# Attention blocks on one Trainium2 core: V loaded from ScalarE's queue, wo by column halves, wq and the second x in small pieces, remainder tiles of 90 steps transposed by DMA

## The chip, the cores and the metric

The kernel runs on one core of one Trainium2 chip. TensorE (PE in the profile) does the matmuls, VectorE (DVE), ScalarE (ACT) and GpSimd (POOL) work beside it, and SyncE (SP) issues most DMAs. The metric is the device time of one execution in microseconds (us); lower is better.

## The reference: what is computed

Two independent grouped-query attention blocks, A and B, of the same shape; their outputs stand side by side in the last dimension. Everything is bf16.

```python
B, Sq, D = 16, 80, 576
Hq, Hkv, Sk, Dh = 32, 16, 512, 128
q = (x @ wq).reshape(B, Sq, Hq, Dh).transpose(0, 2, 1, 3)
k = jnp.repeat(k_cache, 2, axis=1)
v = jnp.repeat(v_cache, 2, axis=1)
scores = jnp.einsum("bhqd,bhkd->bhqk", q, k) * (Dh ** -0.5)
p = softmax(scores, axis=-1)
o = jnp.einsum("bhqk,bhkd->bhqd", p, v)
out = o.transpose(0, 2, 1, 3).reshape(B, Sq, Hq * Dh) @ wo
```

Each K and V head serves two query heads, that is 160 query rows (2 x 80) against 512 keys.

## The kernel before

**Units and tiles.** A unit U is one batch row with four K/V heads; there are 64 units in each problem, 128 in all (A is U = 0 to 63). A unit's 4 x 160 query rows make five tiles of 128 rows: tiles k = 1 to 4 hold the first 128 rows of each head, and the remainder tile k = 0 holds the last 32 rows of all four. A tile's work: scores of 128 x 512 by PE (line 658; line 644 for the remainder, four matmuls of 32 columns of the array side by side), the row maximum by VectorE (667), the exponential with row sums by ScalarE (671), a reciprocal by VectorE (677), the scaling of P by GpSimd (680), and four 128 x 128 transposes by PE (686) with a copy out of PSUM by VectorE (692 for the remainder, 694 for the others). P transposed (pT) is then multiplied with V (line 731, four matmuls of 160 columns for a head), and ScalarE copies the product to oT (747).

**The remainder tile by DMA.** In some units the four transposes and the copy of tile k = 0 are replaced by one DMA transpose from p_sb into pT (line 698), issued by SyncE. `RDMA`, `RPER` and `RSKIP` choose the units: U from 24 to 125 with U % 4 equal to 1 or 3, without 50 to 61, 45 in all. In these units the reciprocal is made in two parts, tile 0 alone and tiles 1 to 4 together (`RG`).

**Around the units.** Eight units share a q projection (an "octet"): 16 groups of five matmuls (540) whose results ScalarE or VectorE copy to qT (551, 552). Its wq part, 576 x 1024, is loaded for every second octet (lines 514 and 517), and used for both halves of the batch. Every 32 units a block of 16 heads of oT is multiplied with wo in 20 output blocks of 128 x 288 (line 781, 16 matmuls each), two column halves (c3) for each of ten row blocks (r); before, the two halves of a row block follow each other. The first result of a problem goes to acc, the last is added to acc (809) and stored (815). x of problem A is transposed by PE, x of problem B by four DMA transposes (481, 485).

**What sets the order.** The order on every engine is written out ahead by a planner (`_Sched`) in the program: every operation has a key (its wished time in steps), a stream in which order is kept, a duration, the buffers that it reads and writes, and for a DMA a `cost`. `arrange` plays the operations through on a model of the engines, with one DMA queue for all (`dma_free`) and a landing time `DLAT`; each engine takes the operation with the smallest key among those that are ready. `finalize` turns the buffers' dependences into semaphore waits. Scores run `LA` = 10 tiles ahead of the products. There are 5 buffers for K, 4 for V, 3 for pT, 12 for P.

**Queues.** SyncE issues all loads (K by DMA transpose at line 612, V by plain DMA at 616, wo in four parts of four heads at 580, wq, x), the remainder transposes and the stores, in one queue. ScalarE issues only the first four wq pieces.

The lines that the change and the steps below touch:

Of the kernel before, what the change touches and what calls it, by code (L numbers as in the profile page):

```python
# [22 lines left out]
KC = 2.95  # L23
VK = 8.0
KK = 8.0
DLAT = 1.6
XC = 0.4
QL2 = 10.0
VC = 1.65
WQC = 3.2  # L30
NQ = 3
NWS = 4
# [6 lines left out]
NML = 12  # L39
XDMA = True  # L40
RG = (((0, 1, 2, 3, 4),), ((0,), (1, 2, 3, 4)))
RDMA = (24, 126)
RPER = (1, 3)
RSKIP = ((50, 62),)
XK = (15.0, 15.0)
WQK = 4.0
WQKB = 4.0
RDC = 0.78
# [11 lines left out]
XH = -2.0  # L60
WQ1 = -16.8
OPX = ((12.0, 1.8), (18.5, 1.45), (18.5, 1.45), (18.5, 1.45))
# [3 lines left out]
WOL = 1.2  # L66
WOA = (99.0, 99.0, 99.0, 99.0)
WOS = 1.0
# [19 lines left out]
class _Op:  # L88
    __slots__ = ("engs", "eng", "key", "seq", "emit", "reads", "writes", "dsem", "stream", "dur", "lat", "cost",
                 "alloc", "pri", "after", "pre", "start", "done", "mode",  # L90
                 "deps", "signals", "sidx", "waits", "clock", "name")


class _Sched:
# [10 lines left out]
    def add(self, eng, key, emit, reads=(), writes=(), dsem=None, name="", stream=None, dur=0.1, lat=0.15,  # L105
            cost=0.0, alloc=(), mode=0, ahead=0.0, after=None):
# [5 lines left out]
        op.after = after  # L112
        op.seq = len(self.ops)
# [21 lines left out]
    def arrange(self):  # L135
        ops = sorted(self.ops, key=lambda o: (o.key, o.seq))
        last_w, readers = {}, {}
        for op in ops:
# [19 lines left out]
            op.pre = list(deps.values())  # L158
        streams = {}
# [11 lines left out]
        dma_free = 1.4  # L171
# [14 lines left out]
        def ready(o, now):  # L186
            t = 0.0
            if o.after is not None:
                d = self.marks[o.after]
                if d.start is None:  # L190
                    return None
                t = d.start
            for d in o.pre:
                if d.done is None:
                    return None
                if not (d.eng == "pe" and o.engs[0] == "pe"):
                    t = max(t, d.done)
            if o.alloc:
# [6 lines left out]
        while left:  # L205
# [30 lines left out]
            if o.dsem is not None:  # L236
                d0 = max(st + 0.5, dma_free)
                dma_free = d0 + o.cost
                o.done = dma_free + DLAT
            else:  # L240
                o.done = st + dur + o.lat
# [82 lines left out]
def bass_concat_heads__gqa_block_cached__gqa_block_cached__near_ridge_kernel(  # L324
# [27 lines left out]
    with ExitStack() as es:  # L352
# [11 lines left out]
        wo_sb = sb("wo_sb", [128, NWS * (HH // NWC), D], BF16)  # L364
# [10 lines left out]
        sem_names = (["e_pe", "e_act", "e_dve", "e_pool", "d_x00", "d_x01", "d_x10", "d_x11", "d_wo",  # L375
# [100 lines left out]
        for half in range(NPP):  # L476
            x_ap = probs[1][0]

            def em_ldxt(e, x_ap=x_ap, half=half):
                src = x_ap.rearrange("b s d -> (b s) d")[half * NROW:(half + 1) * NROW, :]  # L480
                return e.dma_start_transpose(xT[:, half, 0:4, :], src[:, 0:512].rearrange("n (c d) -> n c d", c=4))

            def em_ldxt4(e, x_ap=x_ap, half=half):
                src = x_ap.rearrange("b s d -> (b s) d")[half * NROW:(half + 1) * NROW, :]
                return e.dma_start_transpose(xT[:, half, 4:5, :],
                                             src[:, D - 128:D].rearrange("n (c d) -> n c d", c=1))

            k_ = 5.0 * (UPR + 16 * half - lead[NG // 2 + 2 * half]) - XK[half]
            S.add("sp", k_, em_ldxt, writes=[R(("xT", half, b_), 1) for b_ in range(NRT)], dsem="d_x%d0" % half,
                  name="ldxt%d" % half, stream="x", dur=4.7, cost=3.5)  # L490
            S.add("sp", k_ + 0.01, em_ldxt4, writes=[R(("xT", half, "t"), 1)], dsem="d_x%d0" % half,
                  name="ldxtb%d" % half, stream="x", dur=1.4, cost=0.9)

        QB = ((0, 6), (6, 2))
        for goct in range(NG):
# [7 lines left out]
            for pi, (c0, c1) in enumerate(pieces):  # L503
                t_ld = 5.0 * (u0 - lead[goct]) - (WQKB if goct == NG // 2 else WQK)
                if goct < 2:
                    t_ld = (-90.0, WQ1)[goct] + (10.0, 0.02)[goct] * pi
                fr = (c1 - c0) / 1024.0
                dsem = "d_wqs" if goct == 0 and pi == 0 else "d_wqt" if goct == 1 and pi == 0 else "d_wq%d" % wsl
                eng = "act" if goct == 0 else "sp"
                strm = "wqa" if goct == 0 else "wq"  # L510

                def em_ldwa(e, wq_ap=wq_ap, q=q, wsl=wsl, c0=c0, c1=c1):
                    src = wq_ap[0:512, q * 1024 + c0:q * 1024 + c1]
                    return e.dma_start(wq_sb[:, wsl, 0:4, c0:c1], src.rearrange("(c p) n -> p c n", p=128))

                def em_ldwb(e, wq_ap=wq_ap, q=q, wsl=wsl, c0=c0, c1=c1):
                    return e.dma_start(wq_sb[64:128, wsl, 4, c0:c1],
                                       wq_ap[512:576, q * 1024 + c0:q * 1024 + c1])

                wr = [pi] if len(pieces) == 2 else [0, 1]  # L520
                S.add(eng, t_ld, em_ldwa, writes=[R(("wq", wsl, "a", p_), wv) for p_ in wr], dsem=dsem,
                      name="ldwa%d.%d" % (goct, pi), stream=strm, dur=0.5, cost=WQC * fr)
                S.add(eng, t_ld + 0.01, em_ldwb, writes=[R(("wq", wsl, "b", p_), wv) for p_ in wr], dsem=dsem,
                      name="ldwb%d.%d" % (goct, pi), stream=strm, dur=0.5, cost=0.6 * fr)

            for i in range(8):
                for c in range(2):
# [27 lines left out]
                    if prob:  # L555
                        xr.append(R(("xT", half, "t"), 1))
                    S.add("pe", x, em_qp,
                          reads=[R(("wq", wsl, s_, i // 4), wv) for s_ in "ab"] + [R(("wqz",), 0)] + xr,
# [9 lines left out]
        for prob in range(2):  # L568
            wo_ap = probs[prob][4]
            hc = HH // NWC  # L570
            for hh in range(NPAIR):
                for wc in range(NWC):
# [322 lines left out]
```

## Time and profile before

| | |
|---|---|
| median of 3 runs | 782.39 us (781.14 to 784.07) |
| the profiled execution | 780.9 us |
| its span, first to last instruction | 779.2 us |
| PE busy | 772.0 us, 99% of the span |
| VectorE busy | 678.6 us, 87% |
| ScalarE busy | 611.6 us, 78% |
| GpSimd busy | 432.4 us, 55% |
| DMA moved | 166.44 MB, mean 214 GB/s |
| SyncE's queue (q1), share of the 16 DMA engines' span | 95.7% |
| granted clock of PE | 1.00 |

The span is what the instructions of the profiled execution cover; 1.7 us of its time lie around it. A DMA share over 1 means that several packets of an engine overlap in the record. A group of instructions is told as line, engine, operation, out<-in, count, then its busy time, the mean of one in ns, and the idle time of the engine before it with what ended most of it. "SPq" and "ACTq" are the queues of SyncE and ScalarE that issue DMAs; the length of an issue includes its waits.

### The profile page before, as it was taken

To read this page: it belongs to the slowest core of one execution; us is meant where nothing else is said; L and a number is where in the kernel's file an instruction comes from. 1 tells how busy PE (TensorE), PEld (TensorE's weight loads), DVE (VectorE), ACT (ScalarE), POOL (GpSimd) and SP (SyncE) were. 2 spreads that over 40 slices of the span, in tenths; PEclk is the share of its full clock that TensorE was granted. 3 is DMA by queue.
4 is the path that set the end of the run, shared out by engine and by line. 5 is a ranking of instruction groups with operands and counts; after the bars stand their busy time and mean duration, and the time that the engine had idled before them with its cause. 6 is when DMAs were issued, how large, how long until landed. Compare 5 with 4: busy or idle time off the path is not lost.

```text
span 779.2 us, 21256 instructions
## 1 busy us (share of the span) xinstructions
PE 772.0 (99%) x8078; PEld 567.5 (73%) x8078; DVE 678.6 (87%) x1558; ACT 611.6 (78%) x1736; POOL 432.4 (55%) x647
## 2 busy tenths in 40 slices
PE   9999999999999999999999999999999999999998
PEld 5576677777777777767777777777777777777786
DVE  4999988888888899888898899988888888989982
ACT  1878988888888888867787777978888887887860
POOL 1555755565655656555655655655655655664660
PEclk9999999999999999999999999999999999999999
DMA  9999999988899999999999999999999978999951
GB/s 249 226 259 240 249 222 247 203 188 197 205 200 213 204 237 247 251 213 227 211 229 214 177 214 244 258 218 237 221 230 202 200 177 196 257 220 210 187 134 32
DMA packets 386564, 166.44 MB, mean 214 GB/s; under 512 B 300576, under 2 KB 383008, under 8 KB 386464
## 3 DMA queue, kind: packets, MB, share of 16 engines
q1 hardware_dynamic: 385248, 163.91, 95.7%
q8 instruction: 65, 1.06, 0.6%
q10 hardware_dynamic: 1216, 1.18, 0.5%
q14 instruction: 35, 0.29, 0.1%
HBM read 87.46 MB, written 2.95 MB: 116 GB/s over the span
## 4 chain that ended last, share of the span: by engine, by line
PE 91%; DVE 7%; DMA 1%; ACT 0%; POOL 0%; issue 0%; SPq 0%
PE ps L540 20%; PE ps L781 20%; PE ps L731 17%; PE ps L686 15%; PE ps L658 13%; DVE negmax L667 4%; PE ps L644 4%; DVE pT L694 2%; DVE qT L552 1%; DMA kT<-in_A_k_cache_dram 1%; PE ps L409 0%; PE ps L464 0%; DVE pT L692 0%; ACT p_sb L671 0%; PE ps L424 0%; POOL p_sb L680 0%
## 5 line engine op out<-in xcount | busy, mean ns | idle before, releaser
L680 POOL TENSOR_SCALAR p_sb<-p_sb,rinv 128x512 bf16<-128x512 bf16 x640 | 430.0, 692 | 325.5 <-DVE rinv L677 325.1
L671 ACT ACTIVATE p_sb<-ps,negmax 128x512 bf16<-128x512 f32 x640 | 441.3, 693 | 84.0 <-DVE negmax L667 77.1
L667 DVE TENSOR_REDUCE negmax<-ps 128x1 f32<-128x512 f32 x640 | 427.8, 679 | 9.6 <-PE ps L658 5.1
L686 PE MATMUL ps<-ident,p_sb 128*128 128x128 bf16 x2380 | 229.7, 219 | 1.1 <-POOL p_sb L680 0.5
L694 DVE COPY pT<-ps 128x512 bf16<-128x512 bf16 x512 | 209.9, 413 | 16.4 <-PE ps L686 14.2
L731 PE MATMUL ps<-pT,v_sb 128*128 128x160 bf16 x2048 | 222.6, 233 | 0.1
L540 PE MATMUL ps<-xT,wq_sb 128*128 128x480 bf16 (+1 forms) x1280 | 213.2, 300 | 0.1
L731 PEld LDWEIGHTS ps<-pT,v_sb 128*128 128x128 bf16 x2048 | 158.4, 98 | 54.3 <-ACT oT L747 5.9
L686 PEld LDWEIGHTS ps<-ident,p_sb 128*128 128x128 bf16 x2380 | 168.7, 98 | 35.7 <-DVE pT L694 6.5
L658 PE MATMUL ps<-kT,qT 128*128 128x512 bf16 x512 | 189.0, 379 | 0.6 <-ACT p_sb L671 0.6
L781 PE MATMUL ps<-wo_sb,oT 128*128 128x288 bf16 x1280 | 171.5, 286 | 0.0
L540 PEld LDWEIGHTS ps<-xT,wq_sb 128*128 128x128 bf16 x1280 | 106.9, 98 | 61.4 <-ACT oT L747 2.6
L781 PEld LDWEIGHTS ps<-wo_sb,oT 128*128 128x128 bf16 x1280 | 122.8, 98 | 34.8 <-ACT qT L551 1.3
L747 ACT CAST oT<-ps 128x320 bf16<-128x320 f32 x256 | 108.7, 425 | 37.0 <-PE ps L731 36.6
L671 ACT ACTIVATION_READ_ACCUMULATOR p_sb<-ps,negmax 128x1 f32 x640 | 130.1, 203 | 0.0
L551 ACT ACTIVATE qT<-ps 128x160 bf16<-128x160 f32 (+1 forms) x159 | 63.2, 398 | 25.9 <-PE ps L540 24.9
L552 DVE TENSOR_SCALAR qT<-ps 128x480 bf16<-128x480 f32 (+1 forms) x97 | 54.7, 564 | 22.2 <-PE ps L540 21.1
L658 PEld LDWEIGHTS ps<-kT,qT 128*128 128x128 bf16 x512 | 49.2, 98 | 6.3 <-ACT p_sb L671 3.1
L809 DVE TENSOR_TENSOR osb<-ps,acc 128x288 bf16<-128x288 f32 x40 | 18.2, 456 | 27.6 <-PE ps L781 27.4
L644 PE MATMUL ps<-kT,qT 128*32 128x512 bf16 x512 | 39.6, 384 | 1.1 <-DMA kT<-in_A_k_cache_dram 0.9
L677 DVE RECIPROCAL rinv<-rowsum 128x1 f32<-128x1 f32 (+1 forms) x173 | 29.6, 171 | 11.1 <-ACT p_sb L671 11.1
L692 DVE COPY pT<-ps 128x512 bf16<-128x512 bf16 x83 | 34.5, 416 | 4.9 <-PE ps L686 4.7
(19 smaller groups left out, 47.0 us busy)
## 6 DMA issues: line engine op xcount, KB each, us to landing
v_sb<-in_A_v_cache_dram SPq DMA_DIRECT2D x64, 512.0 KB, 4.6
v_sb<-in_B_v_cache_dram SPq DMA_DIRECT2D x64, 512.0 KB, 4.6
wo_sb<-in_A_wo_dram SPq DMA_DIRECT2D x8, 576.0 KB, 7.6
wo_sb<-in_B_wo_dram SPq DMA_DIRECT2D x8, 576.0 KB, 7.4
wq_sb<-in_B_wq_dram SPq DMA_DIRECT2D x4, 1024.0 KB, 6.7
out_dram<-osb SPq DMA_DIRECT2D x40, 72.0 KB, 2.3
wq_sb<-in_A_wq_dram SPq DMA_DIRECT2D x2, 1024.0 KB, 7.4
wq_sb<-in_A_wq_dram ACTq DMA_DIRECT2D x2, 512.0 KB, 6.9
```

What stands on the lines that cost most here:

```text
L540: last = e.matmul(ps[:, vb.phys, 0:n1 - n0], lhsT=wq_sb[:, wsl, ck, i * 128:(i + 1) * 128], rhs=xT[:, half, ck, n0:n1], start=(ck == 0), s ...
L551: return e.activation(dst, src, AF.Identity, scale=SCALE)
L644: last = e.matmul(ps[32 * g4:32 * g4 + 32, vb_.phys, :], lhsT=qT[:, qsl_, bl_, g4 * 160 + 128:g4 * 160 + 160], rhs=kT[:, ks_, :, g4 * 128: ...
L658: return e.matmul(ps[:, vb.phys, :], lhsT=qT[:, qsl, bl, gl * 160:gl * 160 + 128], rhs=kT[:, ks, :, gl * 128:(gl + 1) * 128], start=True, ...
L667: return e.tensor_reduce(negmax[:, si:si + 1], ps[:, vb.phys, :], axis=AX.X, op=AluOpType.max, negate=True)
L671: return e.activation(p_sb[:, psl, :], ps[:, vb.phys, :], AF.Exp, bias=negmax[:, si:si + 1], scale=1.0, accum_out=rowsum[:, ss, k:k + 1])
L680: return e.tensor_scalar(p_sb[:, psl, :], p_sb[:, psl, :], rinv[:, ss, k:k + 1], 1.0, op0=AluOpType.mult, op1=AluOpType.mult)
L686: last = e.transpose(psb[:, vt.phys, j * 128:(j + 1) * 128], p_sb[:, psl, j * 128:(j + 1) * 128], ident[:])
L694: return e.tensor_copy(pT[:, pts, :, 0:4, gl * 32:gl * 32 + 32], psb[:, vt.phys, 0:512].rearrange("p (j h c) -> p j h c", j=4, h=4))
L731: last = e.matmul(ps[:, vo.phys, off:off + 160], lhsT=v_sb[:, vs, gl, j * 128:(j + 1) * 128], rhs=pT[:, pts, j, :, gl * 32:gl * 32 + 32], ...
L747: return e.copy(dst, src)
L781: last = e.matmul(ps[:, vb.phys, 0:DC], lhsT=oT[:, hi, rb * 128:(rb + 1) * 128], rhs=wo_sb[:, wi, c3 * DC:(c3 + 1) * DC], start=(hi == 0), ...
```

## The change

V's loads move to ScalarE's queue, at a place that the planner sets `VLAG` = 2.0 us after their buffer is free; the first four are released by named operations. The planner's DMA model gets two queues that share the engines (`dma_end`), with other costs. wo is kept as 16 heads of full width as before, but loaded in two column halves of four parts each, each released by the position of the units, and the output blocks run by column half first (but for the last half of problem B's batch). wq parts after those of the first two octets are loaded in five pieces of 128 rows (the last of 64), each released two units after the one before, and x of problem B in five DMA transposes for each half, also two units apart. The remainder tile goes by DMA in all units of 24 to 45, in units 46 to 69 with U % 4 equal to 1 or 3, and in all units of 70 to 125: 90 units. The number of buffers and all other operations stay.

The diff, cut to its core:

```diff
-KC = 2.95
+KC = 2.1
...
-DLAT = 1.6
+DLAT = 0.6
...
-VC = 1.65
-WQC = 3.2
+VC = 1.75
+WQC = 3.1
...
-NWS = 4
...
+VENG = "act"
+VDUR = 0.42
+VN = 1
+VLAG = 2.0
+VK0 = (0.0, 0.0, 0.0, 0.0)
+VAF = ("qp0.3.1", "qp0.7.0", "qp0.7.1", "qk6")
+STENG = "sp"
+WENG = "sp"
+WOENG = "sp"
+QLAT = 1.25
+QRING = 1.45
+WOC = 1.05
...
-RDMA = (24, 126)
-RPER = (1, 3)
-RSKIP = ((50, 62),)
-XK = (15.0, 15.0)
-WQK = 4.0
-WQKB = 4.0
-RDC = 0.78
+RSEL = ((24, 46, (0, 1, 2, 3)), (46, 70, (1, 3)), (70, 126, (0, 1, 2, 3)))
+RDC = 0.72
...
-XH = -2.0
+XH = 0.0
...
+WQ1B = 0.02
...
-WOL = 1.2
-WOA = (99.0, 99.0, 99.0, 99.0)
-WOS = 1.0
+WOR = (((4.0, 1.5), (12.0, 1.5)), ((9.5, 2.0), (17.0, 1.0)), ((9.5, 2.0), (17.0, 1.0)), ((9.5, 2.0), (17.0, 1.0)))
+WQR = (-12.0, 2.0)
+XR = (-14.0, 2.0)
...
+def dma_end(e, st, cost, free):
+    d0 = max(st + QLAT, free.get(e, 0.0))
+    oth = [q for q in free if q != e]
+    w = max(0.0, free[oth[0]] - d0) if oth else 0.0
+    if cost <= w:
+        end = d0 + 2 * cost
+        free[oth[0]] += cost
+    else:
+        end = d0 + cost + w
+        if w:
+            free[oth[0]] = d0 + 2 * w
+    free[e] = end
+    return end, free
...
-                d0 = max(st + 0.5, dma_free)
-                dma_free = d0 + o.cost
-                o.done = dma_free + DLAT
+                t_, fe = dma_end(e, st, o.cost, dma_free)
+                o.done = t_ + DLAT
+                free[e] = max(free[e], t_ - (QRING if o.xp else 8.0))
...
-            def em_ldxt(e, x_ap=x_ap, half=half):
-                src = x_ap.rearrange("b s d -> (b s) d")[half * NROW:(half + 1) * NROW, :]
-                return e.dma_start_transpose(xT[:, half, 0:4, :], src[:, 0:512].rearrange("n (c d) -> n c d", c=4))
-            def em_ldxt4(e, x_ap=x_ap, half=half):
-                src = x_ap.rearrange("b s d -> (b s) d")[half * NROW:(half + 1) * NROW, :]
-                return e.dma_start_transpose(xT[:, half, 4:5, :],
-                                             src[:, D - 128:D].rearrange("n (c d) -> n c d", c=1))
-            k_ = 5.0 * (UPR + 16 * half - lead[NG // 2 + 2 * half]) - XK[half]
-            S.add("sp", k_, em_ldxt, writes=[R(("xT", half, b_), 1) for b_ in range(NRT)], dsem="d_x%d0" % half,
-                  name="ldxt%d" % half, stream="x", dur=4.7, cost=3.5)
-            S.add("sp", k_ + 0.01, em_ldxt4, writes=[R(("xT", half, "t"), 1)], dsem="d_x%d0" % half,
-                  name="ldxtb%d" % half, stream="x", dur=1.4, cost=0.9)
+            st0 = UPR + 16 * half - lead[NG // 2 + 2 * half]
+            for ck in range(5):
+                def em_ldxt(e, x_ap=x_ap, half=half, ck=ck):
+                    src = x_ap.rearrange("b s d -> (b s) d")[half * NROW:(half + 1) * NROW, :]
+                    c0 = ck * 128 if ck < 4 else D - 128
+                    return e.dma_start_transpose(xT[:, half, ck:ck + 1, :],
+                                                 src[:, c0:c0 + 128].rearrange("n (c d) -> n c d", c=1))
+                S.add("sp", 5.0 * st0 - 20.0 + 0.01 * ck, em_ldxt,
+                      writes=[R(("xT", half, b_), 1) for b_ in range(NRT)] if ck == 0 else [R(("xT", half, "t", ck), 1)],
+                      dsem="d_x%d0" % half, name="ldxt%d.%d" % (half, ck), stream="x", dur=0.7, cost=0.85, xp=True,
+                      after=int(4 * (st0 + XR[0] + XR[1] * ck)))
...
-                t_ld = 5.0 * (u0 - lead[goct]) - (WQKB if goct == NG // 2 else WQK)
-                if goct < 2:
-                    t_ld = (-90.0, WQ1)[goct] + (10.0, 0.02)[goct] * pi
+                st0 = u0 - lead[goct]
+                t_ld = 5.0 * st0 - 20.0 if goct > 1 else (-90.0, WQ1)[goct] + (10.0, WQ1B)[goct] * pi
...
-                eng = "act" if goct == 0 else "sp"
+                eng = "act" if goct == 0 else WENG
...
-                def em_ldwa(e, wq_ap=wq_ap, q=q, wsl=wsl, c0=c0, c1=c1):
-                    src = wq_ap[0:512, q * 1024 + c0:q * 1024 + c1]
-                    return e.dma_start(wq_sb[:, wsl, 0:4, c0:c1], src.rearrange("(c p) n -> p c n", p=128))
-                def em_ldwb(e, wq_ap=wq_ap, q=q, wsl=wsl, c0=c0, c1=c1):
-                    return e.dma_start(wq_sb[64:128, wsl, 4, c0:c1],
-                                       wq_ap[512:576, q * 1024 + c0:q * 1024 + c1])
-                wr = [pi] if len(pieces) == 2 else [0, 1]
-                S.add(eng, t_ld, em_ldwa, writes=[R(("wq", wsl, "a", p_), wv) for p_ in wr], dsem=dsem,
-                      name="ldwa%d.%d" % (goct, pi), stream=strm, dur=0.5, cost=WQC * fr)
-                S.add(eng, t_ld + 0.01, em_ldwb, writes=[R(("wq", wsl, "b", p_), wv) for p_ in wr], dsem=dsem,
-                      name="ldwb%d.%d" % (goct, pi), stream=strm, dur=0.5, cost=0.6 * fr)
+                for k0, k1 in (((0, 4), (4, 5)) if goct < 2 else ((0, 1), (1, 2), (2, 3), (3, 4), (4, 5))):
+                    def em_ldw(e, wq_ap=wq_ap, q=q, wsl=wsl, c0=c0, c1=c1, k0=k0, k1=k1):
+                        if k0 == 4:
+                            return e.dma_start(wq_sb[64:128, wsl, 4, c0:c1],
+                                               wq_ap[512:576, q * 1024 + c0:q * 1024 + c1])
+                        src = wq_ap[k0 * 128:k1 * 128, q * 1024 + c0:q * 1024 + c1]
+                        return e.dma_start(wq_sb[:, wsl, k0:k1, c0:c1], src.rearrange("(c p) n -> p c n", p=128))
+                    S.add(eng, t_ld + 0.01 * k0, em_ldw,
+                          writes=[R(("wq", wsl, ck, p_), wv) for ck in range(k0, k1)
+                                  for p_ in ([pi] if len(pieces) == 2 else [0, 1])], dsem=dsem,
+                          name="ldw%d.%d.%d" % (goct, pi, k0), stream=strm, dur=0.5,
+                          cost=(0.12 + 0.2 * WQC * (k1 - k0) if k0 < 4 else 0.4) * fr,
+                          after=int(4 * (st0 + WQR[0] + WQR[1] * k0)) if goct > 1 else None)
...
-        for prob in range(2):
+        for sg in range(2 * NPAIR):
+            prob, hh = divmod(sg, NPAIR)
...
-            for hh in range(NPAIR):
-                for wc in range(NWC):
-                    h0 = hh * HH + wc * hc
-                    ci = (prob * NPAIR + hh) * NWC + wc
-                    wos = ci % NWS
-                    x = 5.0 * (prob * UPR + hh * NPP * 16 + OPX[2 * prob + hh][0]) - WOL * (NWC - wc)
-                    def em_ldwo(e, wo_ap=wo_ap, h0=h0, hc=hc, wos=wos):
-                        src = wo_ap[h0 * 128:(h0 + hc) * 128, :]
-                        return e.dma_start(wo_sb[:, wos * hc:(wos + 1) * hc, :],
-                                           src.rearrange("(h p) n -> p h n", p=128))
-                    S.add("sp", x, em_ldwo, writes=[R(("wo", wos), ci)] + ([R(("warm",), 3), R(("ones",), 1)] if ci == 0 else []),
-                          dsem="d_wo", name="ldwo%d.%d.%d" % (prob, hh, wc), stream="wo", dur=0.5, cost=2.0,
-                          after=None if WOA[2 * prob + hh] > 50 else 4 * (prob * UPR + hh * NPP * 16)
-                          + int(4 * (OPX[2 * prob + hh][0] - WOA[2 * prob + hh] + WOS * wc)))
+            base = prob * UPR + hh * NPP * 16
+            for n in range(2 * NWC):
+                i_, wc = divmod(n, NWC)
+                c3 = (sg + i_) % 2
+                h0 = hh * HH + wc * hc
+                def em_ldwo(e, wo_ap=wo_ap, h0=h0, hc=hc, wc=wc, c3=c3):
+                    src = wo_ap[h0 * 128:(h0 + hc) * 128, c3 * DC:(c3 + 1) * DC]
+                    return e.dma_start(wo_sb[:, wc * hc:(wc + 1) * hc, c3 * DC:(c3 + 1) * DC],
+                                       src.rearrange("(h p) n -> p h n", p=128))
+                w0, ws_ = WOR[sg][i_]
+                o0_, os_ = OPX[sg] if sg < 3 else (LP0, LPS)
+                S.add(WOENG, 5.0 * (base + o0_ + (0.0, 5 * os_)[i_]) - 1.2 * (NWC - wc), em_ldwo,
+                      writes=[R(("wo", c3, wc), sg)]
+                      + ([R(("warm",), 3 + c3), R(("ones",), 1 + c3)] if sg == 0 and wc == 0 else []),
+                      dsem="d_wo%d" % c3, name="ldwo%d.%d.%d" % (sg, c3, wc), stream="wo", dur=0.5, cost=WOC,
+                      after=int(4 * (base + w0 + ws_ * wc)))
...
-                src = vc_ap[b, 4 * q:4 * q + 4, :, :].rearrange("g (p j) d -> p g (j d)", j=4)
-                return e.dma_start(v_sb[:, vs, :, :], src)
+                src = vc_ap[b:b + VN, 4 * q:4 * q + 4, :, :].rearrange("b g (p j) d -> p b g (j d)", j=4)
+                return e.dma_start(v_sb[:, vs:vs + VN, :, :], src)
...
-                  dsem="d_k%d" % ks, name="ldk%d" % U, stream="K", dur=3.4, cost=KC)
-            S.add("sp", 5.0 * U - VK, em_ldv, writes=[R(("V", vs), U)],
-                  dsem="d_v%d" % vs, name="ldv%d" % U, stream="V", dur=0.45, cost=VC)
+                  dsem="d_k%d" % ks, name="ldk%d" % U, stream="K", dur=1.8, cost=KC, xp=True)
+            if U % VN == 0:
+                S.add(VENG, VK0[U] if U < 4 and VK0[U] else 5.0 * U - VK, em_ldv, writes=[R(("V", vs + i_), U + i_) for i_ in range(VN)],
+                      dsem="d_v%d" % vs, name="ldv%d" % U, stream="V", dur=VDUR, cost=VN * VC, lag=VLAG,
+                      after=VAF[U] if U < 4 else None)
...
-            rdma = RDMA[0] <= U < RDMA[1] and U % 4 in RPER and not any(a_ <= U < b_ for a_, b_ in RSKIP)
+            rdma = any(a_ <= U < b_ and U % 4 in m_ for a_, b_, m_ in RSEL)
...
-                          name="rtr%d" % T, stream="RT", dur=RDD, cost=RDC, ahead=RDO)
+                          name="rtr%d" % T, stream="RT", dur=RDD, cost=RDC, ahead=RDO, xp=True)
...
-                        r, c3 = divmod(n, NOC)
+                        last = hh == NPAIR - 1
+                        sg = prob * NPAIR + hh
+                        base = prob * UPR + hh * NPP * 16
+                        if prob == 1 and last and half:
+                            r, c3 = divmod(n, NOC)
+                        else:
+                            c3, r = divmod(n, NRT)
+                            c3 = (c3 + half + sg) % 2
...
-                        base = prob * UPR + hh * NPP * 16
-                        last = hh == NPAIR - 1
...
-                            o0_, os_ = OPX[2 * prob + hh]
+                            o0_, os_ = OPX[sg]
...
-                        ci0 = (prob * NPAIR + hh) * NWC
...
-                            def em_op(e, rb=rb, c3=c3, vb=vb, sp_=sp_, ci0=ci0):
+                            def em_op(e, rb=rb, c3=c3, vb=vb, sp_=sp_):
...
-                                    wi = (ci0 + hi // hc) % NWS * hc + hi % hc
...
-                                                    rhs=wo_sb[:, wi, c3 * DC:(c3 + 1) * DC],
+                                                    rhs=wo_sb[:, hi, c3 * DC:(c3 + 1) * DC],
...
-                                  reads=ot_reads + [R(("wo", c_ % NWS), c_) for c_ in range(ci0, ci0 + NWC)],
+                                  reads=ot_reads + [R(("wo", c3, wc), sg) for wc in range(NWC)],
...
```

`lag` is added to an operation's ready time once what it waits for is done; `xp` marks DMA transposes, which hold their issuing engine in the plan until `QRING` before their end.

## The prediction

> **What bounds the kernel now.** I read the page's first part, then the chain of work that ended last, then the groups of instructions. Three lines settle the question of the engine:
>
> ```profile
> PE 772.0 (99%) x8078; PEld 567.5 (73%) x8078; DVE 678.6 (87%) x1558; ACT 611.6 (78%) x1736; POOL 432.4 (55%) x647
> PE 91%; DVE 7%; DMA 1%; ACT 0%; POOL 0%; issue 0%; SPq 0%
> L686 PE MATMUL ps<-ident,p_sb 128*128 128x128 bf16 x2380 | 229.7, 219 | 1.1 <-POOL p_sb L680 0.5
> ```
>
> TensorE (PE) is busy for 772.0 of 779.2 us and carries 91% of the chain; the other engines have 13% to 45% of the span free. A busy PE need not be a PE at its pace, so I looked at the starts in the timeline (columns: start, length, engine, line, count):
>
> ```profile
> 304.52 0.39 PE L686 MATMUL ps<-ident,p_sb 128*128 128x128 bf16 x4
> 304.74 0.38 PE L658 MATMUL ps<-kT,qT 128*128 128x512 bf16 x1
> 304.96 0.44 PE L731 MATMUL ps<-pT,v_sb 128*128 128x160 bf16 x4
> 305.23 0.38 PE L658 MATMUL ps<-kT,qT 128*128 128x512 bf16 x1
> ```
>
> The lengths overlap, and the starts give the price: four transposes hold PE for 0.22 us (304.52 to 304.74), one 512-column score matmul for 0.22, four 160-column matmuls for 0.27. In the whole trace the starts of consecutive transposes lie 56 ns apart, so a tile of four costs 0.225 us. PE streams like this from 16 us to the end: the 7.2 us in which it is not busy are 1.4 before 20 us, 1.9 between 20 and 100, 1.0 between 320 and 340, 2.7 after 760 (the last store among them).
>
> The second question is who comes next. SyncE issues nearly all DMAs, and its queue's timeline shows no pause:
>
> ```profile
> 503.49 3.56 SPq L612 DMA_TRANSPOSE kT<-in_B_k_cache_dram  x1
> 507.15 1.22 SPq L698 DMA_TRANSPOSE pT<-p_sb  x1
> 508.41 0.58 SPq L616 DMA_DIRECT2D v_sb<-in_B_v_cache_dram  x1
> 509.04 3.73 SPq L612 DMA_TRANSPOSE kT<-in_B_k_cache_dram  x1
> 512.81 0.58 SPq L616 DMA_DIRECT2D v_sb<-in_B_v_cache_dram  x1
> 513.44 3.73 SPq L612 DMA_TRANSPOSE kT<-in_B_k_cache_dram  x1
> ```
>
> Two units with one remainder transpose take 9.95 us of this queue, one unit without takes 4.4. PE spends 5.8 us a unit (scores of unit 70 start at 419.8 us, of unit 126 at 743.5). So the DMA queue is close behind PE. Matching each K load's landing with the first matmul that needs it: mostly 10 to 20 us ahead in units 24 to 48 and 98 to 116 (there the issue waits for the K buffer to come free), but 0.3 us ahead in units 53 and 57 and 0.7 in unit 87, where wq and x, or wo, are loaded in a lump.
>
> **Part 1: 45 more remainder tiles by DMA.** Before, units 24 to 125 with an odd number, without 50 to 61, are 45. After, 22 (24 to 45) + 12 (odd ones of 46 to 69) + 56 (70 to 125) = 90. Removed: 45 tiles x 4 transposes x 56 ns = 10.1 us of PE, all of it on the path, since PE waits for nothing there. Every other matmul stays in number and shape. Also removed: 45 copies L692 of 416 ns = 18.7 us of VectorE; added: 45 reciprocals in two parts (155 + 170 ns) instead of one (181 ns), 6.5 us. VectorE's net 12 us lie beside PE and are priced at nothing. GpSimd's 640 normalisations stay. **Sum on the path: -10.1 us.**
>
> **Part 2: V from ScalarE's queue.** SyncE loses 128 issues of 0.58 us (75 us). ScalarE gets them; its own queue shows the price:
>
> ```profile
> 0.79 0.49 ACTq L514 DMA_DIRECT2D wq_sb<-in_A_wq_dram  x1
> 1.32 0.56 ACTq L517 DMA_DIRECT2D wq_sb<-in_A_wq_dram  x1
> 1.92 0.59 ACTq L514 DMA_DIRECT2D wq_sb<-in_A_wq_dram  x1
> ```
>
> 128 x 0.58 = 74 us, so ScalarE goes from 612 to 686 of 769 us, 89%. Behind a waiting V load stand the exponentials, and behind them the score banks and PE. The load waits for the last product of the unit four before; the planner holds it 2.0 us after that, and scores run some 10 tiles ahead of the products, so a short wait is covered. Cover is thinnest early:
>
> ```profile
> 20.00:140.00 120.00, 118.14 (x1237) 83.23 (x1236) 111.45 (x248) 100.16 (x289) 69.76 (x104) 1.00 1.08 240
> 540.00:660.00 120.00, 119.88 (x1257) 89.20 (x1256) 103.62 (x237) 97.27 (x277) 67.77 (x102) 1.00 0.95 205
> ```
>
> (Busy us of PE, PEld, DVE, ACT, POOL in a stretch, then clock, DMA share, GB/s.) From 20 to 140 us VectorE is 93% busy, ScalarE 83%; 21 V issues add 12.2 us and make it 94%, and no remainder tile goes by DMA there. Bounds: 0 if the lead absorbs it, 12.2 us if every issue delays PE. The nearest row is PE's own idle time in that stretch, 1.9 us with VectorE already at 93%; I take 0 and keep both ends.
>
> **Part 3: what the DMA engines can do.** 45 tiles of 128 KB add 5.9 MB to 166.4. In one queue each costs 1.25 us (1.21 and the gap); at the rate of the K packets, 0.45 us. Windows around one K load show why the two prices differ:
>
> ```profile
> 62.75:64.00 1.25, 1.25 (x15) 0.92 (x14) 1.03 (x3) 1.00 (x4) 1.25 (x2) 1.00 1.28 290
> 64.25:65.00 0.75, 0.72 (x5) 0.40 (x5) 0.71 (x3) 0.25 (x1) 0.57 (x1) 1.00 0.41 69
> 65.50:66.00 0.50, 0.50 (x9) 0.07 (x8) 0.49 (x1) 0.00 (x0) 0.50 (x2) 1.00 1.03 358
> 7.00:9.00 2.00, 1.81 (x28) 1.60 (x27) 1.15 (x4) 0.19 (x1) 0.00 (x0) 1.00 1.07 374
> ```
>
> K's packets run at 290 GB/s, V's at 358, but where the queue passes from K to V the engines move 69 GB/s at a share of 0.41 for some 0.75 us; after a remainder tile (498.0 to 499.25 us) it is 7 GB/s for 1.25 us. A second queue may fill these holes: from 7 to 9 us ScalarE's wq and SyncE's x run together at 374 GB/s, half each by packets. With the holes filled a unit costs 0.524 MB / 290 + 0.524 / 358 + 0.131 / 290 = 3.7 us; without, 4.4 + 1.25 = 5.65. No row shows plain copies of one queue beside transposes of the other in steady work, so the bounds for the DMA side are 0 and the second rival's price; I take 0, by the 374 GB/s row, since the holes are in the queue's order and not in the engines' rate.
>
> **Part 4: wo, wq and x in pieces.** Same bytes, spread. SyncE issues 16 more wo, 18 more wq pieces (0.6 us each, 20 us), x in ten transposes for 12 us as before; against the 75 us given up, and 57 for the new tiles, its queue is even. Output blocks of one column half come first; matmuls are the same 1280. The gain is at most PE's idle 1.0 us at 320 to 340 us, where a K load is the releaser in the chain. The first four V loads are released by q projections and the first scores, which PE runs from 8 us on, instead of going out from 18 to 35 us; three of them at 1.4 us each meet K loads that have little to spare: loads 1 to 3 land 1.7, 3.2 and 1.0 us early. Bounds: -3 us (all PE idle of 20 to 100 and 320 to 340 us gone) and +3 us; value 0, as nothing there is sized by a row.
>
> **Sum.** 780.9 us (the profiled execution; span 779.2 and 1.7 around it) - 10.1 = 770.8. It lies 1.5 below the median of the runs, 782.39; on that footing 782.4 - 10.1 = 772.3. **I predict 772 us.**
>
> **Rivals.**
>
> *ScalarE takes PE's place early.* The 12.2 us come through in part, or V loads wait in its queue longer than planned. For it: 93% and 94% in one stretch. Against: a lead of ten tiles, and copies of q that either engine may take. A quarter to three quarters, 3 to 9 us: 775 to 781.
>
> *The two queues do not add up (slower).* If V in its own queue fills no holes, units 70 to 125 need 56 x 5.65 = 316 us, and two wq loads (1.18 MB, 3.3 us at 358), two wo loads (2.36 MB, 6.6) and some 15 stores (0.5) another 27: 343. PE needs 323.7 - 28 x 0.225 = 317. The 26 us less the 10 to 14 us that K is ahead at unit 70 come out as PE waits: 12 to 16 us, and 0 to 5 more in units 24 to 45 (124 + 13 against 123, 14 ahead). Together about 17: 772 + 17 = 789, in a range of 784 to 795. It decides once a unit costs over 5.2 us of DMA. For it: the queue's timeline has no pause now, and the landings of unit 53. Against: the 0.41 window. The Trainium skill's page "DMA: Bandwidth & Descriptors", section "Rules for kernel authors", says that spreading DMAs over several issuing engines doesn't help bandwidth, as they share the same 16 engines, and saves issue time alone. By that rule this rival's 789 us would be the forecast; the traced holes speak against reading it so, as they are time in which the shared engines stood still.
>
> *PE's waits go as well.* The full -3 us of part 4: 766 to 769.
>
> **How the numbers follow.** Forecast (769 to 775) 0.60; ScalarE early 0.16; queues don't add up 0.12; waits gone too 0.12. The range takes in the forecast, the first rival and most of the last: 767 to 781. Within 0.5% (778.5 to 786.3, about what a measurement of this kernel tells from no change) falls the upper part of the first rival and the lower edge of the second: 0.08. Faster 0.81, slower 0.11.
>
> **What would show it.** Right: transposes L686 down by 180 from 2380, PE still busy over 98%, span near 769; the K-load share of SyncE's queue shorter, pauses in it; DMA share over 0.8 where it is now 0.41. ScalarE in error: PE's weight loads waiting for the exponential or the maximum in total over 3 us, in 20 to 140 us. Queues in error: score matmuls waiting for kT, or products for pT, from unit 100 on. A PE stalled behind late remainder tiles (landing 2.5 us now, once they share the engines with V) would make all of it wrong.

## The result, and the profile after

The changed kernel takes 795.93 us (median of 4 runs, 795.28 to 797.29), beside 783.23 (781.14 to 784.64) for the kernel before on the same chip: a ratio of 1.0167 with an interval of 1.0137 to 1.0196. It is slower, by about 13 us, where I had forecast 10 us less. The profiled execution took 795.28 us, with a span of 793.5; before it was 780.9 and 779.2. Here and below a median is of all runs of a kernel, while a ratio leaves out single runs more than 1.5% above that kernel's fastest and compares with the kernel before on the same chip.

The page of the kernel after: busy time by engine, the chain of waits, the transposes, and two lines of the DMA issues (count, KB each, median us from issue to landing).

```profile
PE 769.6 (97%) x7898; PEld 559.5 (71%) x7898; DVE 680.2 (86%) x1591; ACT 604.7 (76%) x1703; POOL 432.4 (54%) x647
PE 80%; DVE 12%; DMA 3%; ACT 2%; SPq 2%; issue 1%; POOL 0%; ACTq 0%
L715 PE MATMUL ps<-ident,p_sb 128*128 128x128 bf16 x2200 | 212.9, 220 | 0.6 <-POOL p_sb L709 0.3
v_sb<-in_A_v_cache_dram ACTq DMA_DIRECT2D x64, 512.0 KB, 5.3
pT<-p_sb SPq DMA_TRANSPOSE x90, 4.7
```

The transposes are gone as planned (2200 instead of 2380), but PE now stands still for 23.9 us of the span instead of 7.2. DMA and SyncE's queue, 1% of the chain before, hold 5%. A remainder tile lands 4.7 us after its issue; before it was 2.5:

```profile
pT<-p_sb SPq DMA_TRANSPOSE x45, 2.5
```

The next view cuts the span in stretches (busy us of PE, PEld, DVE, ACT, POOL, then clock, DMA share, GB/s), and shows that the loss isn't spread:

```profile
320.00:400.00 80.00, 73.46 (x760) 54.56 (x759) 66.10 (x151) 56.53 (x160) 40.34 (x60) 0.98 1.07 221
400.00:480.00 80.00, 80.00 (x832) 58.65 (x831) 73.05 (x174) 62.51 (x176) 44.60 (x67) 1.00 1.09 217
480.00:560.00 80.00, 72.41 (x723) 52.18 (x722) 62.93 (x152) 57.77 (x164) 43.36 (x65) 0.96 1.12 230
```

Between 400 and 480 us PE never rests. On either side it loses 6.5 and 7.6 us, where before it was busy for 79.04 and 79.93:

```profile
320.00:400.00 80.00, 79.04 (x839) 58.62 (x837) 71.07 (x162) 61.94 (x177) 45.81 (x69) 1.00 1.04 224
480.00:560.00 80.00, 79.93 (x847) 58.88 (x843) 71.57 (x167) 65.42 (x187) 47.67 (x71) 1.00 1.04 232
```

In the first of these two stretches the kernel after issues four parts of wo, five of wq, four of the second x and eight stores on top of K, V and the tiles, in the second seven parts of wo and eight of wq. Between them there are ten stores, but only one part each of wo, wq and x.

To place the loss, I compared the start of the first score matmul of a unit in the two traces (after minus before, us):

| unit | 5 | 24 | 48 | 56 | 64 | 80 | 92 | 98 | 126 | end |
|---|---|---|---|---|---|---|---|---|---|---|
| after | +5.4 | +3.8 | +2.9 | +0.9 | +9.0 | +7.8 | +17.2 | +15.9 | +14.4 | +14.4 |

There are three steps: the start (+5.4), units 56 to 64 (+8.1), units 80 to 92 (+9.4). In the rest the kernel holds or gains a little.

**One stall, read step by step.** SyncE's queue in the kernel after (start, length, operation). The remainder of unit 59 was normalised by GpSimd at 357.0 us, and its pT buffer was free at 359.8:

```profile
357.16 8.59 SPq L639 DMA_TRANSPOSE kT<-in_A_k_cache_dram  x2
365.80 0.60 SPq L538 DMA_DIRECT2D wq_sb<-in_B_wq_dram  x1
366.44 0.58 SPq L847 DMA_DIRECT2D out_dram<-osb  x1
367.06 2.15 SPq L511 DMA_TRANSPOSE xT<-in_B_x_dram  x1
369.25 3.74 SPq L639 DMA_TRANSPOSE kT<-in_A_k_cache_dram  x1
373.09 1.21 SPq L727 DMA_TRANSPOSE pT<-p_sb  x1
```

Its transpose is the last line: it waited 13.3 us while the queue issued the lines above it, and landed at 378.06. PE at that time (the bracket is PE's idle time ahead of the instruction):

```profile
374.38 0.38 PE L687 MATMUL ps<-kT,qT 128*128 128x512 bf16 x1
378.11 0.71 PE L760 MATMUL ps<-pT,v_sb 128*128 128x160 bf16 x4 [3.35 <-DMA pT<-p_sb]
378.61 0.63 PE L715 MATMUL ps<-ident,p_sb 128*128 128x128 bf16 x4
382.44 0.39 PE L715 MATMUL ps<-ident,p_sb 128*128 128x128 bf16 x4
```

PE waits 3.35 us. Then the same four transposes take 0.63 us instead of 0.39, because the granted clock has dropped:

```profile
377.25:381.00 3.75, 2.89 (x22) 2.59 (x22) 1.44 (x3) 0.76 (x2) 0.00 (x0) 0.54 0.97 200
```

Twelve of the 90 tiles land at most 0.2 us ahead of the first product that needs them; the view of waits names DMA for only two of these, and ScalarE, VectorE or "issue" for others (the 2.82 us at 501.26 are put down to the exponential L700). Where a line of that view names an engine that had long been done, the landings have to be matched with the products.

**The account.** PE's idle time grows from 7.2 to 23.9 us: +16.7. The clock falls to half four times, for 3.41 us each, so at most +6.8. The transposes bring -10.1. Sum +13.4, of +14.3 measured between the spans; the rest is not accounted for.

### The profile page after: what moved, and what is told of

The parts are those of the page before. It is cut to its first block, busy times and chain, and to the rows that moved or that the text cites. A ratio compares the mean times of both kernels' runs of the same rounds, so it can differ in the third digit from the quotient of the medians.

```text
span 793.5 us, 20970 instructions
## 1 busy us (share of the span) xinstructions
PE 769.6 (97%) x7898; PEld 559.5 (71%) x7898; DVE 680.2 (86%) x1591; ACT 604.7 (76%) x1703; POOL 432.4 (54%) x647
## 4 chain that ended last, share of the span: by engine, by line
PE 80%; DVE 12%; DMA 3%; ACT 2%; SPq 2%; issue 1%; POOL 0%; ACTq 0%
PE ps L813 20%; PE ps L564 18%; PE ps L760 15%; PE ps L715 13%; PE ps L687 11%; DVE negmax L696 7%; PE ps L673 4%; DVE pT L723 3%; ACT p_sb L700 2%; DVE qT L576 1%; DMA kT<-in_A_k_cache_dram 1%; DMA pT<-p_sb 1%; SPq L639 1%; SPq L477 0%; DVE pT L721 0%
## 5 line engine op out<-in xcount | busy, mean ns | idle before, releaser
L700 ACT ACTIVATE p_sb<-ps,negmax 128x512 bf16<-128x512 f32 x640 | 440.6, 692 | 92.8 <-DVE negmax L696 83.3
L723 DVE COPY pT<-ps 128x512 bf16<-128x512 bf16 x512 | 210.6, 413 | 29.3 <-PE ps L715 28.5
L715 PE MATMUL ps<-ident,p_sb 128*128 128x128 bf16 x2200 | 212.9, 220 | 0.6 <-POOL p_sb L709 0.3
L687 PE MATMUL ps<-kT,qT 128*128 128x512 bf16 x512 | 191.7, 382 | 0.0
L715 PEld LDWEIGHTS ps<-ident,p_sb 128*128 128x128 bf16 x2200 | 156.2, 98 | 36.8 <-DVE pT L723 6.3
L700 ACT ACTIVATION_READ_ACCUMULATOR p_sb<-ps,negmax 128x1 f32 x640 | 129.0, 202 | 0.0
L576 DVE TENSOR_SCALAR qT<-ps 128x480 bf16<-128x480 f32 (+1 forms) x130 | 72.1, 555 | 20.5 <-PE ps L564 18.9
L575 ACT ACTIVATE qT<-ps 128x160 bf16<-128x160 f32 (+1 forms) x126 | 47.5, 377 | 27.2 <-PE ps L564 26.8
L706 DVE RECIPROCAL rinv<-rowsum 128x1 f32<-128x1 f32 (+2 forms) x218 | 35.4, 165 | 4.5 <-ACT p_sb L700 4.3
L825 ACT COPY acc<-ps 128x288 f32<-128x288 f32 x40 | 15.7, 393 | 5.4 <-PE ps L813 4.9
```

The lines of the kernel that those rows point to most:

```text
L576: return e.tensor_scalar(dst, src, SCALE, None, op0=AluOpType.mult)
L687: return e.matmul(ps[:, vb.phys, :], lhsT=qT[:, qsl, bl, gl * 160:gl * 160 + 128], rhs=kT[:, ks, :, gl * 128:(gl + 1) * 128], start=True, ...
L700: return e.activation(p_sb[:, psl, :], ps[:, vb.phys, :], AF.Exp, bias=negmax[:, si:si + 1], scale=1.0, accum_out=rowsum[:, ss, k:k + 1])
L715: last = e.transpose(psb[:, vt.phys, j * 128:(j + 1) * 128], p_sb[:, psl, j * 128:(j + 1) * 128], ident[:])
L723: return e.tensor_copy(pT[:, pts, :, 0:4, gl * 32:gl * 32 + 32], psb[:, vt.phys, 0:512].rearrange("p (j h c) -> p j h c", j=4, h=4))
```

## The experiments

Two theories at first. **Late tiles**: SyncE's queue and the DMA engines can't carry 90 remainder tiles in time. **V's queue**: V on ScalarE's queue is what delays the rest. Later two forms of the first: **capacity** (too many bytes in the engines where wo and wq load) and **order** (the planned place in SyncE's queue is wrong).

**One part at a time.** First the changed kernel with 45 tiles, the kernel before with 90, and the changed kernel with V back on SyncE:

```diff
# e1_a45tiles, on the kernel after
-RSEL = ((24, 46, (0, 1, 2, 3)), (46, 70, (1, 3)), (70, 126, (0, 1, 2, 3)))
+RSEL = ((24, 50, (1, 3)), (62, 126, (1, 3)))
# e2_b90tiles, on the kernel before (RSEL as in the kernel after)
-            rdma = RDMA[0] <= U < RDMA[1] and U % 4 in RPER and not any(...)
+            rdma = any(a_ <= U < b_ and U % 4 in m_ for a_, b_, m_ in RSEL)
# e3_avsp, on the kernel after
-VENG = "act"
+VENG = "sp"
```

> The changed kernel with the 45 remainder tiles by DMA of the kernel before (odd units of 24 to 125 without 50 to 61) in place of 90; all else as changed. Theory 'late tiles' (the added tiles sit in stretches where wo, wq and x load too, land late, PE waits for them and its clock drops): PE gets its 10.1 us of transposes back and loses the waits of the middle; the loss of the first 40 us, some 5 us, stays: 785 to 790. Rival 'V's queue' (V's packets take turns with K and the tiles and delay both, whatever their number): the waits stay, 796 to 806.

> The kernel before with the 90 remainder tiles of the change; V, wo, wq and x as before. 'Late tiles': 773 by PE's work plus waits as large as the changed kernel's or larger, as one queue has less room: 790 to 800. 'V's queue': K and the tiles are alone with a V that stands in line, and the gain comes: 772 to 778.

> The changed kernel with V's loads issued by SyncE, in SyncE's queue; all else as changed, 90 tiles. 'Late tiles': not better than 795. 'V's queue': 772 to 780.

Measured: e1 787.38 us (ratio 1.011, 1.0065 to 1.0155); e2 801.38 (1.0256, 1.0218 to 1.0293); e3 817.69 (1.0428, 1.0375 to 1.0482). V's queue falls as the only cause: with V back on SyncE the 90 tiles cost far more, not less. Late tiles stand (e2 is even 1.4 us above the upper end of their range). But e1, with no more tiles than before, still loses 1.1%, and its one long wait isn't for a tile (PE's timeline of e1):

```profile
318.61 2.98 PE L813 MATMUL ps<-wo_sb,oT 128*128 128x288 bf16 x16 [4.02 <-DMA wo_sb<-in_A_wo_dram]
```

So V's queue and the pieces have prices of their own. The next runs take V's queue alone, the pieces alone, and the start alone:

```diff
# e4_bvact, on the kernel before
-            S.add("sp", 5.0 * U - VK, em_ldv, writes=[R(("V", vs), U)],
+            S.add("act", 5.0 * U - VK, em_ldv, writes=[R(("V", vs), U)],
# e10_a45vsp, on the kernel after: RSEL of e1, and
-VENG = "act"
+VENG = "sp"
# e5_vlate, on the kernel after
-VAF = ("qp0.3.1", "qp0.7.0", "qp0.7.1", "qk6")
+VAF = ("qk3", "qk8", "qk9", "qk16")
```

> The kernel before with V's loads issued by ScalarE and nothing else changed. 'Late tiles': V's queue alone costs little, 781 to 787, ScalarE some 85% busy. 'V's queue': 790 or more, with waits of PE for kT and pT and landings of the tiles at 4 us or more.

> The changed kernel with the 45 tiles of the kernel before and V in SyncE's queue: what is left of the change is wo by column halves and wq and x in pieces. If the pieces are harmless: 780 to 786. If they lengthen SyncE's queue (each piece 0.4 to 0.6 us to issue, and more passages between transposes and copies): 790 or more, with PE waiting for tiles and wo between units 48 and 64 and 80 and 92.

> The changed kernel with the first four V loads released later, about where the kernel before issued them (after scores 3, 8, 9 and 16 of the plan); all else as changed. Theory 'start' (V's early loads share the engines with wq and K and cost 3 to 5 us in the first 40 us): unit 5's scores start at 38 to 40 us instead of 43.1 and the time is 791 to 793. If the start's loss has another cause: 796.

e4: 800.47 us (1.0245, 1.0222 to 1.0268), 13 us above the upper end that late tiles gave, and in the range of the rival: V's queue alone costs time as well. It loses in three places: 6.7 us at the start, where the first four V loads go out at 3.5 to 7.5 us, ahead of SyncE's wq pieces (from 11.45 us) and of all K loads but the first (from 15.51); a wait of 2.92 us for a tile at 317.0; one of 6.24, again for a tile, at 698.6. Between units 10 and 48 it loses only 1.1 us. Its 45 tiles land in 5.3 us (2.5 before): V in a queue of its own delays them.

e10: 793.11 us (1.0141, 1.0112 to 1.0171). Without the tiles and V's queue the rest of the change (the pieces, the order of the output blocks, the planner's new costs) is no help: PE waits for parts of wo (4.03 us at 314.8, 2.69 at 509.0) and for tiles (1.74, 1.42, 1.24).

e5: 794.96 us (789.57 to 799.17; 1.0159, 1.0094 to 1.0224). In its trace the start is mended, unit 5 at +0.8 instead of +5.4, but the total can't be told from the kernel after, since the two later steps eat it. So the traces point at the early V loads as what delays the start, by an amount that is not fixed: four kernels with the same early V loads stand at +5.4 (after), +3.1 (e1), +10.1 and +2.6 (e6 and e7, below) at unit 5, those with later ones at +0.8 (e5) to +2.4 (e10). By the time it is inconclusive.

Together, as ratios to the kernel before (tiles and V with neither pieces nor later V loads was not run, and the planner's costs change with the pieces, so the columns aren't strictly additive):

| | before's loads | pieces |
|---|---|---|
| 45 tiles, V on SyncE | 1 | 1.014 |
| 90 tiles, V on SyncE | 1.026 | 1.043 |
| 45 tiles, V on ScalarE | 1.025 | 1.011 |
| 90 tiles, V on ScalarE | not run | 1.017 |

Each part alone costs time. The 45 more tiles, which take 1.3% off PE, bring nothing even in their best company: 1.017 against 1.011, with intervals that overlap.

**Bytes or order?** If the engines are short only where wo and wq load, fewer bytes there must bring the gain back. e6 loads a quarter of wo in units 80 to 92, e7 a quarter of V from unit 24 on, and e8 tells the planner dearer loads, so that it plans another order:

```diff
# e6_wo2q
...
+                    hn = 1 if sg == 2 else hc
-                    src = wo_ap[h0 * 128:(h0 + hc) * 128, c3 * DC:(c3 + 1) * DC]
+                    src = wo_ap[h0 * 128:(h0 + hn) * 128, c3 * DC:(c3 + 1) * DC]
...
# e7_vq
+                gn = 4 if U < 24 else 1
-                src = vc_ap[b:b + VN, 4 * q:4 * q + 4, :, :].rearrange("b g (p j) d -> p b g (j d)", j=4)
+                src = vc_ap[b:b + VN, 4 * q:4 * q + gn, :, :].rearrange("b g (p j) d -> p b g (j d)", j=4)
...
# e8_costs
-KC = 2.1
+KC = 2.95
...
-DLAT = 0.6
+DLAT = 1.6
```

> The changed kernel; the eight wo loads of the third block (heads 0 to 15 of problem B) bring one head of four, a quarter of the bytes, so the output leaves out most of that wo; order and instructions the same. Theory 'capacity in bursts' (between units 80 and 92 tiles, K, V and 2.36 MB of wo ask for more than the DMA engines do): the 9.4 us lost there fall to 3 or less, 787 to 791. Rival 'order' (a tile stands behind a K issue that takes 4 to 7 us where the plan has 2, whatever the bytes): 794 to 797.

> The changed kernel; from unit 24 on a V load brings one head of four, 128 KB instead of 512, so the output uses stale V for three heads; order and instructions the same. 'Capacity': PE's waits after unit 24 go and only the start's 4 us stay: 775 to 780. 'Order': 787 or more.

> The changed kernel planned with the K cost and landing time of the kernel before (KC 2.95 and DLAT 1.6 in place of 2.1 and 0.6): the same work and bytes, another order. 'Order': the tiles get their place in time, 775 to 788. 'Capacity': the order cannot help, 793 to 803.

e6: 787.75 us (1.0084, 1.0045 to 1.0123). e7: 773.07 (771.63 to 774.9; 0.9884, 0.9856 to 0.9912). e8: 815.48 (1.0377, 1.0298 to 1.0457). So e6 lies in the range that capacity gave, e7 2 us under it, and e8 above both ranges. The stretch view of e6:

```profile
480.00:560.00 80.00, 79.95 (x831) 58.31 (x828) 72.28 (x176) 66.94 (x192) 48.36 (x73) 1.00 1.11 239
```

and of e7, with its busy line and its tiles:

```profile
PE 762.9 (99%) x7898; PEld 556.7 (72%) x7898; DVE 678.7 (88%) x1591; ACT 603.7 (78%) x1703; POOL 432.4 (56%) x647
...
320.00:400.00 80.00, 80.00 (x846) 59.69 (x845) 73.31 (x169) 62.47 (x178) 45.57 (x68) 1.00 0.90 165
480.00:560.00 80.00, 79.73 (x824) 57.84 (x822) 71.67 (x174) 67.83 (x192) 47.88 (x72) 1.00 1.04 189
...
pT<-p_sb SPq DMA_TRANSPOSE x90, 3.5
```

Fewer wo bytes in one burst mend that burst alone: units 80 to 92 gain 1.3 us instead of losing. Fewer V bytes mend both: PE is busy 99% of a span of 769.9 us, 9.3 less than before, at full clock, and a tile lands in 3.5 us. Every instruction of PE, VectorE, ScalarE and GpSimd is in its place there, so what they do was not the cause; the DMA side is. The e8 run speaks against order, as far as one setting can: dearer loads in the plan made the kernel slower still.

**What a unit costs the DMA engines.** e9 runs the loads alone, in six stretches of 24 units that don't wait for any compute:

```python
# K of SyncE, V of SyncE, V of ScalarE, tile of SyncE
PHASES = ((1, 0, 0, 0), (1, 1, 0, 0), (1, 1, 0, 1), (1, 0, 1, 0), (1, 0, 1, 1), (1, 0, 0, 1))
```

> No attention at all: only the loads, 24 units in each of six stretches, as fast as the DMA engines take them, each buffer's next load waiting for its last; the output is zeros. Stretches: K alone; K and V in SyncE's queue; K, tile and V in SyncE's queue; K in SyncE's queue and V in ScalarE's; K and tile in SyncE's and V in ScalarE's; K and tile. Theory 'holes are filled' (the prediction's): two queues take 3.3 us a unit without and 3.7 with the tile, one queue 4.4 and 5.6. Rival 'no gain from two queues' (transposes and plain copies in flight together slow each other): two queues 4.3 to 5 us without and 5.5 to 6.5 with the tile, so that the tile costs 1.2 us or more wherever V is.

Its windows (us, then engines that do nothing here, clock, DMA share, GB/s), for K alone; K and V in one queue; K, tile and V in one; V's own queue while it lasts, and K's rest; the same with tiles, while V lasts:

```profile
4.00:66.00 62.00, 0.00 (x0) 0.00 (x0) 1.00 1.10 201
66.00:172.00 106.00, 0.00 (x0) 0.00 (x0) 1.00 0.98 237
173.00:309.00 136.00, 0.00 (x0) 0.00 (x0) 1.00 0.88 208
310.00:358.00 48.00, 0.00 (x0) 0.00 (x0) 1.00 1.11 335
360.00:400.00 40.00, 0.00 (x0) 0.00 (x0) 1.00 1.13 213
401.00:450.00 49.00, 0.00 (x0) 0.00 (x0) 1.00 1.12 328
```

From the first issue to the last landing of a stretch, divided by 24 (us a unit):

| | one queue | V in its own |
|---|---|---|
| K alone | 2.68 | |
| K and tile | 3.49 | |
| K and V | 4.43 | 3.80 |
| K, tile and V | 5.70 | 4.83 |

A second queue does fill holes, but a unit with its tile came to 4.83 us, not the 3.7 of my sum: between the theory and its rival. These two prices are averages over an uneven stretch. Nothing held V to K's pace, so V's 24 loads were in after 49 us of 91 (49 of 116 with tiles), and K went on without it. What a unit costs when K, tile and V keep step, as in the kernel, no run shows.

The two queues don't share alike. While V streams (310 to 358 us), the queues read (SyncE's is q1, ScalarE's q10; packets, MB, time of the packets as a share of 16 engines):

```profile
q10 hardware_dynamic: 12648, 12.57, 76.6%
q1 hardware_dynamic: 13923, 3.52, 34.3%
```

About as many packets of each (12,648 of 994 bytes on average, 13,923 of 253), so V gets 262 GB/s and K 73: at these rates a K load takes 7.2 us, alone 2.6. The Trainium skill's page "DMA: Bandwidth & Descriptors", section "Queues, rings and completion order", states that each engine takes turns between the queues with work at the grain of a packet. The trace agrees: nearly equal counts, and bytes (3.6 to 1) nearly in the ratio of the packet sizes (3.9 to 1).

**Is there a better mix?** e11 is the kernel after with V late at the start (as e5) and 53 tiles kept out of the bursts; e12 is the kernel before with 13 more tiles outside the bursts:

```diff
# e11_c55: VAF of e5, and
+RSEL = ((24, 40, (0, 1, 2, 3)), (41, 46, (1, 3)), (62, 70, (1, 3)), (70, 78, (0, 1, 2, 3)), (95, 114, (0, 1, 2, 3)), (115, 120, (1, 3)))
# e12_b58: rdma of e2, and
+RSEL = ((24, 38, (0, 1, 2, 3)), (38, 50, (1, 3)), (62, 100, (1, 3)), (100, 112, (0, 1, 2, 3)), (112, 126, (1, 3)))
```

> The changed kernel with the later first V loads and 53 tiles by DMA, none in units 46 to 61, 78 to 94 and after 119, where the loads of wo, wq and x fall. 'Capacity in bursts': no wait of PE over 2 us, 8 x 0.225 = 1.8 us less transposing than before: 778 to 783. If V in its own queue costs time by itself: 785 to 790.

> The kernel before, V still in SyncE's queue, with 13 more tiles by DMA where its K loads run 10 to 20 us ahead (the even units of 24 to 37 and of 100 to 111); 58 in all. 'Capacity in bursts' (a tile is free of cost where the queue is ahead; a unit with tile takes 5.70 us of the queue against PE's 5.6, so the lead lasts): 13 x 0.225 = 2.9 us less, 778 to 781, ratio 0.995 to 0.998. If tiles in any place make others late: 783 or more.

e11: 783.55 us (1.0003, 0.9964 to 1.0043), its twelve runs falling into six of 778.6 to 780.8 and six of 786.4 to 800.5. Its profiled execution had a span of 777.3 at full clock: with the bursts spared no loss is left, and a gain, if there is one, comes in half of the runs only. e12: 782.1 (1.002, 1.0002 to 1.0039), between what its two theories gave. Neither beats the kernel before, and no other run that computes the whole does.

## Why the prediction was wrong, step by step

**Part 1, -10.1 us of PE: right.** e7 shows it nearly whole: -9.3 us of span, though it is 1.0 behind at unit 24. VectorE's 12 us less did not show: it is busy for 680.2 us (678.6 before), since it makes 130 of the copies to qT instead of 97. That lies beside PE, as priced.

**Part 2, ScalarE, value 0: right.** A V issue on ScalarE took 0.37 us, not 0.58. In e7 the exponentials and V issues are as in the kernel after and PE is busy 99%; the rival "ScalarE takes PE's place early" didn't come about.

**Part 3, the DMA engines, value 0: this step failed.** It took the price of a unit, 3.7 us, from a row where copies of two queues run side by side, and noted that no row showed copies beside transposes. In e9 it came to 4.83 us, averaged over a stretch in which V ran ahead. The other end of my bounds, 5.65 in one queue, is 5.70 measured. What the runs showed in place of a value of 0: the tiles land in 4.7 us instead of 2.5, twelve of the 90 only as their product needs them, and PE stands still 16.7 us longer; with three quarters of V's bytes gone (e7) this goes. Two faults made it worse than a wrong size:

- *An average stood for a burst.* Units 80 to 92 need, by an estimate from e9's price and the 358 GB/s row, 12 x 4.83 + 1.77 MB of wo (4.9 us) + 1.70 MB of wq (4.8 us) = 67.7 us of DMA; PE's time for them is 69.0 before, less 6 x 0.225 = 67.6. By this estimate no slack is left. Units 98 to 126, where eight parts of wo are spread over 28 units, lose nothing.
- *The cushion was K's, and not the tile's.* I credited the DMA side with the 10 to 14 us that K is ahead. A tile can't be loaded ahead: it exists only once GpSimd has normalised it. From there, with its pT buffer free, eight tiles of ten in e7 had 9 to 14 us until their product. In SyncE's queue a tile stands behind K loads, which in units 80 to 92 took 3.95 us to issue at the median and up to 6.8 (3.73 and up to 7.0 before). The median wait of a tile in that queue didn't grow (1.7 us, 3.3 before); its landing did. Of the twelve late tiles seven had waited for 6.7 to 13.3 us, the others for 1.6 to 3.9. The last line of the prediction, that late tiles would make all of it wrong, named this, but gave it no price and no chance.

How much of the later landings comes from V's larger share of the packets and how much from the bytes as such, no run tells apart: e7 lessens both.

**The rival "the two queues do not add up"** had the right side and, at 789 (784 to 795), nearly the size; that the measured 795.93 lies so close above it is partly luck. Its mechanism was half right. The point from which it decides, 5.2 us a unit, was not reached (4.83); the loss came in bursts of the other loads instead of evenly over units 70 to 125, and 9.0 of the 14.4 us were lost before unit 70, at the start and in units 56 to 64. Its sign, waits from unit 100 on, came earlier: the long waits for tiles are those of units 53, 59, 80 and 86. The Trainium skill's rule behind it (page "DMA: Bandwidth & Descriptors", "Rules for kernel authors": spreading over engines doesn't help bandwidth) isn't borne out to the letter, as 4.83 is 15% under 5.70. But it was nearer than my 3.7.

**Part 4, bounds -3 to +3: too narrow.** With the early V loads the kernel after is 5.4 us behind at unit 5 (3.8 at unit 24), with later ones in e5 0.8 (0.5). The pieces, which I had priced by SyncE's issue time only, cost 1.4% in e10, together with the planner's new costs: there the last part of wo that a block needs is issued at 314.37 us, and PE waits for it from 314.83 on. Whether its planned place or the pieces ahead of it made it late, no run tells apart. The rival "PE's waits go as well" didn't come about: they grew.

**Missing: the clock.** I priced a PE wait at its length. Four of the waits cost up to 1.7 us on top (3.41 us at half speed), at most 6.8 in all.

## What to carry to other kernels

Before moving work from a full engine to DMA, ask for each new transfer how early its data exists and how late it may land: a load that can run ahead lives on the average rate, but a transfer of a fresh result lives on the longest queue ahead of it and on its landing time beside all the others. Sum the DMA demand over the stretch with the most other loads, with prices for the very mix of transposes and copies that will run there. When nothing in the trace shows that mix, weight the dear end of the bounds.

## What the runs showed of the hardware

- **The clock falls after short waits, but not by their length alone.** In the kernel after, waits of 1.96, 3.35, 2.82 and 2.54 us were each followed by 3.41 us at clock 0.5, starting 2.5 to 3.7 us after the wait began; waits of 1.79 and 1.64 us were not. But neither were 2.86 us at 321.8 in e5 and 2.69 us at 509.0 in e10. What sorts them is the place of the wait. In each of the 13 traces other than e9's, the clock changes only at multiples of 3.41 us from its first change. Cut into stretches on that grid, 22 stretches at full clock had PE idle for 1.96 us or more, and all 22 were followed by half clock; of the 2934 with less (1.94 at most), 4 were. The waits of e5 and e10 lie across an edge, with 1.84 and 1.02, and 1.37 and 1.31 us idle on its two sides. The Trainium skill's page "TensorE: Matmul & The Clock Gate", section "Why this matters for your kernels", warns of idle gaps over some 3 us; here 1.96 were enough. The 3.41 us are the window of its Part 1.
- **Two queues share by packets, not by bytes.** A queue of 1024-byte packets took 262 GB/s and left 73 to the transposes' 256-byte packets.
- **A remainder tile has no fixed price.** The same 128 KB transpose adds 0.81 us a unit beside K alone, 1.27 in one queue with K and V, and 1.03 with V in its own queue (differences in e9's table).
